# K cache rows of 8 KB with two batches interleaved by partition, and a reciprocal moved ahead of an output sum, in a cached attention kernel

## Chip, cores, metric

One core of a Trainium2 chip. The metric is device time in microseconds (us) of one execution; a lower time is better. A profile comes from one execution; its span, from the first instruction to the last, is some 1.8 us shorter than the device time. Every run quoted as fast ran in the undisturbed state.

## The reference

Two independent blocks A and B of the same shape; the outputs are put side by side.

```python
B, Sq, D = 16, 64, 640;  H, Sk, Dh = 32, 512, 128        # all bfloat16
q = (x @ wq).reshape(B, Sq, H, Dh).transpose(0, 2, 1, 3)
scores = einsum("bhqd,bhkd->bhqk", q, k_cache) * Dh ** -0.5
p = softmax(scores)
o = einsum("bhqk,bhkd->bhqd", p, v_cache)
out = o.transpose(0, 2, 1, 3).reshape(B, Sq, H * Dh) @ wo
```

K and V together are 268 MB and are read once. That makes the kernel a contest between transfers (about 406 GB/s in the profile below) and TensorE (90% busy).

## The kernel before

The work is cut into 128 steps. One step is a group of four heads for a pair of batches. (Where a number of bytes stands with it, a "step of 4 bytes", the word means something else: the distance in memory between two neighbouring columns that a matmul reads.) In each step two loads bring K, one per batch, 128 rows of 4 KB, one for each partition (lane) of the on-chip memory; VectorE transposes K in 32 x 32 blocks of 4-byte elements (pairs of bf16; one transpose of 128 x 1024 elements takes 1.24 us); TensorE multiplies q with it (the score matmuls: q is loaded as weights, K is the moving operand, 512 columns of it in each matmul), ScalarE takes the exp with row sums, VectorE the reciprocal, GpSimd normalises, TensorE transposes the weights, multiplies with V and with wo. Every fourth step VectorE takes over the output of four steps (the output sum: a copy in one half of the cases, an addition in the other). Each engine runs a list sorted by the numbers in `AT`.

```python
kn_ring = sb("kn_ring", [128, NK, 2, 2048], BF16)            # slot, batch, 16 keys x 128
kt_ring = sb("kt_ring", [128, NKT, 2, 16, 2, 32, 2], BF16)   # slot, batch, t, j, key row, pair
...
def em_LDK(e, op):                                            # one batch b of step n
    src = blocks[blk][1][2 * bp + b, h:h + 4].rearrange("h (p t) d -> (h p) (t d)", t=16)
    ins = e.dma_start(kn_ring[:, n % NK, b, :], src)
def em_KT(e, op):
    dst = kt_ring[:, n % NKT, b].rearrange("p t j k two -> p (t j k two)").bitcast(F32)
    ins = e.transpose(dst, kn_ring[:, n % NK, b, :].bitcast(F32))
def em_S(e, op):                                              # 4 x 2 x 4 = 32 matmuls
    for f in range(4):
        for b in range(2):
            for i in range(4):                                # head i in rows 32i..32i+31
                rows = slice(32 * i, 32 * i + 32)
                e.matmul(ps[64 * b:64 * b + 64, i, :], qs_ring[rows, n % NQ, f, b, :],
                         kt_ring[rows, n % NKT, b, :, f // 2, :, f % 2], ...,
                         tile_position=(32 * i, 64 * b))
```

The innermost index of the transposed K is the pair, so a score matmul picks every second bf16: a step of 4 bytes.

## Time and profile before

| | before |
|---|---|
| time, median of 3 | 759.53 us |
| TensorE busy | 682.2 us, 90% |
| VectorE busy | 536.7 us, 71% |
| transfers in the steady part | about 406 GB/s |
| steps 4 to 35 | 21.10 us per four steps |

The prediction reads the main views. Two more rows, of the costliest groups of the kernel before (line, engine, operation, output and inputs with shapes, count; then busy us, mean ns of one; then idle time before them), are needed for the comparison:

```profile
L610 DVE STREAM_TRANSPOSE kt_ring<-kn_ring 128x1024 f32<-128x1024 f32 x256 | 313.6, 1236 | 105.8 <-DMA kn_ring<-in_B_k_cache_dram 70.3
...
L620 PE MATMUL ps<-kt_ring,qs_ring 32*64 32x512 bf16 x4096 | 146.4, 396 | 0.0
```

The score matmuls overlap (the program places them on eight tiles of the array, and 32 of them, 396 ns each, are through in 1.14 us), so the busy time, 146.4 us for 128 steps or 1.14 us a step, is the number to watch, and not the 396 ns of one.

### The profile page before, as it was taken

To read this page: it belongs to the slowest core of one execution; us is meant where nothing else is said; L and a number is where in the kernel's file an instruction comes from. 1 tells how busy PE (TensorE), PEld (TensorE's weight loads), DVE (VectorE), ACT (ScalarE), POOL (GpSimd) and SP (SyncE) were. 2 spreads that over 40 slices of the span, in tenths; PEclk is the share of its full clock that TensorE was granted. 3 is DMA by queue.
4 is the path that set the end of the run, shared out by engine and by line. 5 is a ranking of instruction groups with operands and counts; after the bars stand their busy time and mean duration, and the time that the engine had idled before them with its cause. 6 is when DMAs were issued, how large, how long until landed. Compare 5 with 4: busy or idle time off the path is not lost.

```text
span 757.4 us, 57362 instructions
## 1 busy us (share of the span) xinstructions
PE 682.2 (90%) x26518; PEld 528.0 (70%) x26518; DVE 536.7 (71%) x818; ACT 519.6 (69%) x1559; POOL 404.6 (53%) x580
## 2 busy tenths in 40 slices
PE   4579999999999989999978999899997999999995
PEld 3457777777777767777756776677775777777773
DVE  7437777877767777687756777777675787887873
ACT  2437777777777677767756777777775677777772
POOL 5434555546864544645674455445486556455550
PEclk9979999999999999999999999999999999999997
DMA  8999999999999999999999999999999999999970
GB/s 309 394 399 405 406 406 407 406 405 407 400 395 409 407 408 406 407 407 407 406 394 401 406 407 407 406 405 405 406 403 395 406 408 407 402 409 406 407 294 16
DMA packets 99804, 295.12 MB, mean 390 GB/s; under 512 B 9264, under 2 KB 24112, under 8 KB 99760
## 3 DMA queue, kind: packets, MB, share of 16 engines
q1 hardware_dynamic: 91120, 284.20, 95.7%
q10 hardware_dynamic: 8640, 10.49, 3.8%
q14 instruction: 35, 0.29, 0.1%
q8 instruction: 9, 0.15, 0.1%
HBM read 292.03 MB, written 2.62 MB: 389 GB/s over the span
## 4 chain that ended last, share of the span: by engine, by line
PE 33%; SPq 26%; DMA 19%; POOL 9%; DVE 8%; issue 5%; ACT 0%; POOLq 0%; DVEq 0%; ACTq 0%
SPq L546 12%; POOL pn_sb L670 8%; SPq L557 8%; PE ps L705 8%; PE ps L725 8%; PE ps L597 7%; DMA kn_ring<-in_B_k_cache_dram 6%; PE ps L620 6%; DMA kn_ring<-in_A_k_cache_dram 5%; PE ps L681 5%; SPq L559 5%; DMA v_ring<-in_B_v_cache_dram 5%; DVE pT_sb L691 3%; DMA v_ring<-in_A_v_cache_dram 3%; DVE kt_ring L610 1%
## 5 line engine op out<-in xcount | busy, mean ns | idle before, releaser
L670 POOL TENSOR_SCALAR pn_sb<-p_ring,recip 128x512 bf16<-128x512 bf16 x508 | 342.3, 694 | 322.9 <-DVE recip L654 322.8
L610 DVE STREAM_TRANSPOSE kt_ring<-kn_ring 128x1024 f32<-128x1024 f32 x256 | 313.6, 1236 | 105.8 <-DMA kn_ring<-in_B_k_cache_dram 70.3
L641 ACT ACTIVATE p_ring<-ps 128x512 bf16<-128x512 f32 x512 | 298.7, 598 | 32.1 <-PE ps L620 20.3
L691 DVE COPY pT_sb<-ps 128x1024 bf16<-128x1024 bf16 x258 | 164.6, 679 | 79.5 <-PE ps L681 78.8
L705 PE MATMUL ps<-pT_sb,v_ring 32*128 32x64 bf16 (+1 forms) x14528 | 156.7, 192 | 26.2 <-DMA v_ring<-in_B_v_cache_dram 11.0
L725 PE MATMUL ps<-wo_sb,oT_sb 128*128 128x320 bf16 x1040 | 166.6, 303 | 5.9 <-issue 4.8
L597 PE MATMUL ps<-xT_ring,wqp_sb 128*128 128x128 bf16 x2560 | 166.0, 220 | 6.1 <-POOL xT_ring L586 5.8
L705 PEld LDWEIGHTS ps<-pT_sb,v_ring 32*128 32x128 bf16 (+1 forms) x14528 | 142.1, 92 | 40.6 <-DMA v_ring<-in_B_v_cache_dram 14.1
L597 PEld LDWEIGHTS ps<-xT_ring,wqp_sb 128*128 128x128 bf16 x2560 | 157.4, 114 | 13.0 <-issue 6.0
L713 ACT ACTIVATE oT_sb<-ps 128x256 bf16<-128x256 f32 x260 | 85.6, 381 | 107.0 <-PE ps L705 107.0
L620 PE MATMUL ps<-kt_ring,qs_ring 32*64 32x512 bf16 x4096 | 146.4, 396 | 0.0
L603 ACT ACTIVATE qs_ring<-ps 128x512 bf16<-128x512 f32 x128 | 76.5, 598 | 87.7 <-PE ps L597 87.6
L681 PEld LDWEIGHTS ps<-ident,pn_sb 64*128 64x128 bf16 x4128 | 70.8, 95 | 86.8 <-ACT ps L717 65.6
L725 PEld LDWEIGHTS ps<-wo_sb,oT_sb 128*128 128x128 bf16 x1040 | 91.9, 98 | 43.8 <-issue 5.4
L681 PE MATMUL ps<-ident,pn_sb 64*128 64x64 bf16 x4128 | 84.0, 191 | 26.4 <-POOL pn_sb L670 19.8
L641 ACT ACTIVATION_READ_ACCUMULATOR p_ring<-ps 128x1 f32 x512 | 105.9, 207 | 0.0
L620 PEld LDWEIGHTS ps<-kt_ring,qs_ring 32*64 32x64 bf16 x4096 | 55.1, 104 | 31.3 <-issue 0.5
L654 DVE RECIPROCAL recip<-rowsum 128x3 f32<-128x3 f32 (+1 forms) x256 | 36.1, 158 | 24.5 <-ACT p_ring L641 21.2
L717 ACT ACTIVATE ps<-zeros 128x256 f32<-128x256 bf16 x130 | 51.3, 395 | 0.0
L569 POOL COPY wqp_sb<-ws_sb 128x1280 bf16<-128x1280 bf16 x32 | 39.3, 1260 | 7.5 <-DMA ws_sb<-in_A_wq_dram 7.5
L586 POOL COPY xT_ring<-xs_sb 128x640 bf16<-128x640 bf16 x32 | 23.0, 720 | 3.6 <-PE ps L597 3.6
L576 PE MATMUL ps<-ident,xn_ring 128*128 128x128 bf16 x165 | 14.9, 222 | 4.7 <-DMA xn_ring<-in_A_x_dram 3.5
(26 smaller groups left out, 66.3 us busy)
## 6 DMA issues: line engine op xcount, KB each, us to landing
kn_ring<-in_A_k_cache_dram SPq DMA_DIRECT2D x128, 512.0 KB, 14.1
v_ring<-in_A_v_cache_dram SPq DMA_DIRECT2D x128, 512.0 KB, 13.0
kn_ring<-in_B_k_cache_dram SPq DMA_DIRECT2D x128, 512.0 KB, 15.1
v_ring<-in_B_v_cache_dram SPq DMA_DIRECT2D x128, 512.0 KB, 12.7
ws_sb<-in_B_wq_dram SPq DMA_DIRECT2D x10, 512.0 KB, 15.6
wo_sb<-in_B_wo_dram ACTq DMA_DIRECT2D x8, 640.0 KB, 10.9
ws_sb<-in_A_wq_dram SPq DMA_DIRECT2D x4, 640.0 KB, 10.1
wo_sb<-in_A_wo_dram SPq DMA_DIRECT2D x4, 640.0 KB, 12.5
```

Of the source, the lines that this page charges most:

```text
L546: ins = e.dma_start(kn_ring[:, n % NK, b, :], src)
L597: last = e.matmul(ps[:, 1, f * 128:(f + 1) * 128], w[:, kt, f, :], xT_ring[:, xs, kt, :], start=(kt == 0), stop=(kt == KT - 1))
L603: ins = e.activation(qs_ring[:, op.idx % NQ].rearrange("p f b q -> p (f b q)"), ps[:, 1, :], ACTF.Copy, scale=scale)
L610: ins = e.transpose(dst, kn_ring[:, n % NK, b, :].bitcast(F32))
L620: last = e.matmul(ps[64 * b:64 * b + 64, i, :], qs_ring[rows, n % NQ, f, b, :], kt_ring[rows, n % NKT, b, :, f // 2, :, f % 2], start=(f = ...
L641: ins = e.activation(dst, src, ACTF.Exp, scale=1.0, accum_out=rowsum[:, h:h + 1])
L670: ins = e.tensor_scalar(dst, src, recip[:, h // 4 % NR, i:i + 1], 1.0, ALU.mult, ALU.mult)
L681: last = e.transpose(pt_bank(b)[:, 64 * c:64 * c + 64], pn_sb[rows, c, :], ident[rows, rows], tile_position=(64 * b, 0))
L691: ins = e.tensor_copy(pT_sb[:, b].rearrange("p t q -> p (t q)"), pt_bank(b))
L705: last = e.matmul(ps[:, 4 + i, 64 * b:64 * b + 64], v_ring[rows, n % NV, b, c, :], pT_sb[rows, b, c, :], start=(t == 0 and i < 2), stop=(t ...
L713: ins = e.activation(oT_sb[:, 2 * a:2 * a + 2, :], o_ps[:, 2 * a:2 * a + 2, :], ACTF.Copy)
L725: last = e.matmul(out_ps[:, s, :], oT_sb[:, i, :], wo_sb[:, 4 * j + i, s * NH0:(s + 1) * NH0], start=(j == 0 and i == 0), stop=(j == NJ - ...
```

## The change

Its intent: half as many rows for K, each twice as long, so that the transfers pay half as many fixed costs (an estimate of 12 ns a packet, from the means in the trace of before: 87.9 ns for 2048 B and 163.6 ns for 4096 B). A batch of four heads is then only 64 rows. To keep head i in partitions 32i to 32i+31 for both batches, batch 0 goes to the even partitions and batch 1 to the odd ones. A transposed block therefore has the batches side by side, and the key order of the scores changes, which the exp undoes. Both transposes of a step now wait for both loads, and the second load stands in its list at the time of the first. The second part moves one reciprocal ahead of the output sum.

```diff
-              TE=(1.26, 1.39), ..., OS=2.53, ...
+              TE=(1.26, 1.39), ..., OS=2.545, ...
...
-            add("dve", "KT", (n, b), tk, [("kn", n % cfg.NK, b)], [("kt", n % cfg.NKT, b)])
+            add("dve", "KT", (n, b), tk, [("kn", n % cfg.NK, 0), ("kn", n % cfg.NK, 1)], [("kt", n % cfg.NKT, b)])
-            op = add("sp", "LDK", (n, b), tk - 0.9, [], [("kn", n % cfg.NK, b)])
+            op = add("sp", "LDK", (n, b), n + AT["KT"][0] - 0.9, [], [("kn", n % cfg.NK, b)])
...
-        kt_ring = sb("kt_ring", [128, NKT, 2, 16, 2, 32, 2], BF16)
+        kt_ring = sb("kt_ring", [128, NKT, 32, 2, 16, 2, 2], BF16)
...
-            src = blocks[blk][1][2 * bp + b, h:h + 4].rearrange("h (p t) d -> (h p) (t d)", t=16)
-            ins = e.dma_start(kn_ring[:, n % NK, b, :], src)
+            src = blocks[blk][1][2 * bp + b, h:h + 4].rearrange("h (p t) d -> (h p) (t d)", t=32)
+            dst = kn_ring[b::2, n % NK].rearrange("p a c -> p (a c)")
+            ins = e.dma_start(dst, src)
...
-                                        kt_ring[rows, n % NKT, b, :, f // 2, :, f % 2],
+                                        kt_ring[rows, n % NKT, :, f // 2, :, b, f % 2],
...
-            if h // 4 % NJ in WIDE:
-                return src, dst
-            return (src.rearrange("q (th tl k) -> q tl k th", th=2, tl=8), ...)
+            u = 2 if h // 4 % NJ in WIDE else 4
+            return (src.rearrange("q (u t p) -> q t p u", u=u, p=16), dst.rearrange("q (t p u) -> q t p u", p=16, u=u))
```

With the batch between key row and pair, the score matmuls' step becomes 8 bytes.

More of the change, by code (lines that the diff above doesn't have):

```diff
@@ L32 @@
               EX=(0.21, 0.32, 0.43, 0.54), RC=(0.53, 0.75), NM=(0.56, 0.69, 0.82, 0.95), NMZ=(0.54, 0.55, 0.56, 0.76), TR=1.2,
-              TE=(1.26, 1.39), PV=1.75, OE=(2.0, 2.06), ZO=2.11, OP=2.31, OS=2.53, LDWO=2.6, ST=3.374, WP0=-1.75, WP1=-1.6)
+              TE=(1.26, 1.39), PV=1.75, OE=(2.0, 2.06), ZO=2.11, OP=2.31, OS=2.545, LDWO=2.6, ST=3.374, WP0=-1.75, WP1=-1.6)
 class Op:
@@ L607, in em_KT @@
         def em_KT(e, op):
-            n, b = op.idx
-            dst = kt_ring[:, n % NKT, b].rearrange("p t j k two -> p (t j k two)").bitcast(F32)
-            ins = e.transpose(dst, kn_ring[:, n % NK, b, :].bitcast(F32))
+            n, a = op.idx
+            dst = kt_ring[:, n % NKT, 16 * a:16 * a + 16].rearrange("p t j k b two -> p (t j k b two)").bitcast(F32)
+            ins = e.transpose(dst, kn_ring[:, n % NK, a, :].bitcast(F32))
             return ins, ins
@@ L632, in exp_views @@
             src, dst = ps[:, h % 4, :], p_ring[:, h % NP, :]
-            if h // 4 % NJ in WIDE:
-                return src, dst
-            return (src.rearrange("q (th tl k) -> q tl k th", th=2, tl=8),
-                    dst.rearrange("q (tl k th) -> q tl k th", tl=8, th=2))
+            u = 2 if h // 4 % NJ in WIDE else 4
+            return (src.rearrange("q (u t p) -> q t p u", u=u, p=16), dst.rearrange("q (t p u) -> q t p u", p=16, u=u))
         def em_EX(e, op):
```

## The prediction

The sum: 2.8 + 6.6 + 1.9 + 0.5 = 11.8 us, so 747.7 us, and 748.7 with one microsecond given back. Rival (a): loads of 64 rows into every second partition are slower in themselves.

> **What bounds the kernel now.** I read the page's tenths first, then the windows view over stretches, the waits inside each stretch, and the timeline of one group of four steps. A step is one group of four heads for two batches; there are 128 (the page's 256 transposes, two a step).
>
> ```profile
> PE   4579999999999989999978999899997999999995
> PEclk9979999999999999999999999999999999999997
> DMA  8999999999999999999999999999999999999970
> GB/s 309 394 399 405 406 406 407 406 405 407 400 395 409 407 408 406 407 407 407 406 394 401 406 407 407 406 405 405 406 403 395 406 408 407 402 409 406 407 294 16
> ...
> q1 hardware_dynamic: 91120, 284.20, 95.7%
> ```
>
> The transfers never rest: about 406 GB/s from the third slice to the thirty-eighth. TensorE is at 90% or more in nearly all of them too, at full clock. So two limits lie close together, and the averages do not say which holds where. The starts of the score matmuls (L620) in the timeline do. Steps 4 to 35 (55.8 to 225 us) repeat 5.09, 5.48, 5.44, 5.09 us, 21.10 us per four steps, like clockwork. Steps 36 to 103 (225 to 616 us) are irregular, 391 us for 17 groups of four, 23.0 us each. Steps 104 to 127 are regular again, 21.17 us per four. The windows view over these stretches:
>
> ```profile
> 55.70:225.00 169.30, 166.02 (x6580) 129.57 (x6568) 125.99 (x198) 130.32 (x390) 100.03 (x143) 1.00 1.03 404
> 225.00:616.00 391.00, 355.25 (x13968) 274.99 (x13957) 279.10 (x426) 273.70 (x824) 213.64 (x306) 1.00 1.03 405
> 616.00:742.00 126.00, 122.92 (x4849) 95.33 (x4839) 97.92 (x149) 94.42 (x287) 66.32 (x99) 1.00 0.96 379
> ```
>
> TensorE is busy 98% (166.0 of 169.3), 91% and 98% (122.9 of 126.0). The waits agree. In the middle stretch VectorE waits 96.5 us for K:
>
> ```profile
> DVE kt_ring L610 <- DMA kn_ring<-in_B_k_cache_dram: 65.2, 52, 3.9
> DVE kt_ring L610 <- DMA kn_ring<-in_A_k_cache_dram: 31.3, 34, 2.4
> ```
>
> In the first regular stretch that wait is 0.6 us, and the queue of loads waits for TensorE to free V buffers instead:
>
> ```profile
> SPq L557 <- PE ps L705: 39.9, 21, 3.9
> SPq L559 <- PE ps L705: 22.5, 8, 3.3
> ```
>
> So the middle is set by transfers and the two outer stretches by TensorE. The transfers have little to spare in the first: 404 GB/s there is their pace in the middle.
>
> Why does one step of the regular four take 5.44 and not 5.09? The timeline shows that step and the one after it:
>
> ```profile
> 150.70 1.14 PE L620 MATMUL ps<-kt_ring,qs_ring 32*64 32x512 bf16 x32
> ...
> 152.11 0.64 PE L681 MATMUL ps<-ident,pn_sb 64*128 64x64 bf16 x32 [0.27 <-POOL pn_sb L670]
> ...
> 156.14 1.14 PE L620 MATMUL ps<-kt_ring,qs_ring 32*64 32x512 bf16 x32
> ...
> 157.21 0.64 PE L681 MATMUL ps<-ident,pn_sb 64*128 64x64 bf16 x32
> ...
> 169.38 0.81 DVE L735 COPY acc<-ps 128x640 f32<-128x640 f32 x1
> ...
> 170.11 0.21 DVE L654 RECIPROCAL recip<-rowsum 128x3 f32<-128x3 f32 x2
> ...
> 170.37 2.03 POOL L670 TENSOR_SCALAR pn_sb<-p_ring,recip 128x512 bf16<-128x512 bf16 x3 [3.02 <-DVE recip L654]
> ```
>
> At 152.11 TensorE idled 0.27 us for GpSimd's normalisation; at 157.21 it started 0.07 us before the score matmuls were through. 0.27 + 0.07 is the 0.35 us. The cause stands in the last three lines, the same place one group later: the output sum (L735, 0.81 us) goes ahead of the reciprocal on VectorE, so normalisation begins late. (The 5.48 step has the five extra x transposes, 0.44 us of real work.)
>
> [...] The trace's records of single packets on q1 agree: 87.9 ns mean for 2048 B (16,384 of them), 163.6 ns for 4096 B (59,264), so 75.7 ns per 2 KB and 12.1 ns fixed. [...] The score matmul now steps 4 bytes through K[...]; its 32 matmuls take 1.14 us. The trace has no moving operand at 8 bytes.
>
> **The change, part by part.**
> - *K rows.* A K load of 512 KB is 128 rows of 4 KB now, 64 rows of 8 KB after, into the even or the odd partitions. From the two packet sizes I estimate an 8 KB packet at 163.6 + 2 x 75.7 = 315 ns. Per load: 128 x 163.6 = 20.94 us of one engine against 64 x 315 = 20.16, a saving of 0.78, over 16 engines 0.049 us. Eight K loads per four steps: 0.39 us. All 256 loads: 12.5 us, which is the most that fewer packets can give.
> - *The transposes* keep their count, shape and 1.24 us. But both now wait for both loads; the first used to run while the second load landed (the two start 1.28 us apart where data binds). That is about 1.15 us more from the last landing to the end of transposing. With a median of 13 to 15 us from issue to landing (page, part 6), a deep queue stands ahead of the transfer engines; a later release of a slot shortens it and does not empty it. I count 0 in the steady state.
> - *Score matmuls* read K at a step of 8 bytes[...]. I count 0, with a risk below.
> - *Exp* reads PSUM in 2 or 4 interleaved runs. A quarter of the exps already read two runs at a 256-element step: 597.4 ns against 597.6 for the plain ones. 0.
> - *The reciprocal.* The instruction order shows the reciprocal of three heads ahead of the output sum, that of the fourth behind it. The reciprocal's data are ready at 169.42 (third accumulator read) and VectorE is free at 169.46, so it starts some 0.65 us earlier. The wait of 0.35 us goes; 20.75 us per four steps is left for TensorE. The output sum ends 0.2 us later, at about 170.4, still before the value matmuls at 170.65 that overwrite its bank.
>
> The sum by stretch. First regular: TensorE needs 20.75 for 21.10, and the transfers save 0.39, so both limits move: 8 groups x 0.35 = 2.8 us. Middle: 17 x 0.39 = 6.6 us. Last: 24 steps less the tail, 5.5 groups x 0.35 = 1.9 us. Start-up (to 55.8 us, set by loads): about 16 K loads x 0.049 = 0.8, less some of the later transposing, 0.5 us. Together 11.8 us, 759.5 - 11.8 = 747.7. Since neither limit has slack over the other once both moved, I give one microsecond back: **748.7 us**.
>
> **Rivals.**
> (a) [...] 15% for a loss above 2%.
> (b) *The wider step slows the score matmuls.* TensorE is the bound in 40% of the time. The weight loads of L597, which step 8 bytes, take a median 113 ns against 98 for contiguous ones (L725) of equal shape. A tenth more on 1.14 us is 0.11 us a step, 0.46 per four: it cancels the reciprocal's gain and leaves TensorE at 21.2; the time would be about 753 to 756 us. 20%.
> (c) *Only one part works.* If 4 KB rows were limited by memory and not by packets, only the reciprocal counts: 2.8 + 1.9, about 755 us. The straight line through two packet sizes speaks against it. 10%.
> (d) *The later transposes bite* in the middle, where VectorE waits for K and then copies the transposed weights in order: if the queue is shallower than I read, up to 1 us in some of 68 steps, which takes back much of the 6.6 us.
>
> **Range and chances.** With neither (a) nor (b), 744 to 752. Over 2% faster means under 744.3, which needs more than the 12.5 us of packets, or the reciprocal helping in the middle too: 12%. Over 2% slower is above 774.7 and comes nearly only from (a), plus a little for a strong (b): 16%. The rest, 72%, is within 2%. The range runs from 743.5 to 768, its upper end holding (b), (c), (d) and a mild (a).
>
> **What would show it.** Packets on q1 fall by 16,384 to 74,736; single 8 KB packets last 310 to 320 ns (over 400: rival a). GB/s rises from 406 to about 413 in the middle. The regular four becomes 5.09, 5.48, 5.09, 5.09 and TensorE's idle time for normalisation (19.8 us in 44 waits) falls below 8. Thirty-two score matmuls stay at 1.14 us (over 1.2: rival b). VectorE's waits for K shrink or stay near 100 us; above 150 speaks for (d). A time over 775 us would make the whole account wrong.

## The result, and the profile after

The changed kernel takes 820.75 us (median of 4) against 759.12 for before (median of 4): a ratio of 1.0809, interval 1.079 to 1.0828, so 8.1% slower. Ratios here are the mean time of one kernel's fast runs over the mean of the other's of the same rounds, so not quite the ratio of the medians quoted. The clock was 0.989 in the profiled run.

The same rows of the page of the changed kernel, the tenths and the transfer rate over the 40 slices, the queue, the chain that ended last, and the two groups:

```profile
PE   4689999999999999999999999999999999999995
...
GB/s 318 399 406 409 404 370 346 355 359 338 366 399 411 395 369 374 381 366 365 365 387 405 411 403 386 361 363 380 351 367 400 399 360 354 363 353 348 346 170 14
...
q1 hardware_dynamic: 74736, 284.20, 91.3%
...
PE 96%; issue 2%; DVE 1%; ACT 0%; DVEq 0%
...
L611 DVE STREAM_TRANSPOSE kt_ring<-kn_ring 128x1024 f32<-128x1024 f32 x256 | 302.9, 1222 | 1.0 <-DMA kn_ring<-in_A_k_cache_dram 1.0
L621 PE MATMUL ps<-kt_ring,qs_ring 32*64 32x512 bf16 x4096 | 261.1, 620 | 0.0
```

The last row is the finding. The same 4096 score matmuls are busy for 261.1 us in place of 146.4, and one lasts 620 ns in place of 396. TensorE is at 9 tenths without a gap, the final chain is 96% TensorE, and the transfers have fallen back to 340 to 410 GB/s because the loads wait for TensorE. The waits of the load queue for TensorE show it: over the whole run 464.5 us in these two rows of the changed kernel, against 85.3 us in the same two rows of before (54.9 + 30.4, whole-run view).

```profile
SPq L558 <- PE ps L704: 347.7, 92, 6.5
SPq L560 <- PE ps L704: 116.8, 31, 5.0
```

VectorE's wait for K, 96.5 us in the middle stretch before, is 1.0 us in the whole run (the row of L611 above). One step of the timeline of the changed kernel, the one with the output sum in it (start, duration, engine, line):

```profile
401.26 2.06 PE L621 MATMUL ps<-kt_ring,qs_ring 32*64 32x512 bf16 x32
...
403.25 0.64 PE L680 MATMUL ps<-ident,pn_sb 64*128 64x64 bf16 x32
...
405.33 0.17 DVE L653 RECIPROCAL recip<-rowsum 128x3 f32<-128x3 f32 x1
405.42 0.81 DVE L737 TENSOR_TENSOR out_sb<-acc,ps 128x640 bf16<-128x640 f32 x1
405.60 2.70 POOL L669 TENSOR_SCALAR pn_sb<-p_ring,recip 128x512 bf16<-128x512 bf16 x4 [3.21 <-DVE recip L653]
...
407.55 2.07 PE L621 MATMUL ps<-kt_ring,qs_ring 32*64 32x512 bf16 x32
```

Thirty-two score matmuls take 2.06 us where they took 1.14. The second part of the change does what it was meant to: the reciprocal is ahead of the output sum and GpSimd starts 0.27 us after it, but nothing waits for it any more.

**Where the 61.5 us are** (spans 818.9 and 757.4, from the starts of the score matmuls in the two timelines). Start-up to step 4: 56.9 against 55.7, +1.2. Steps 4 to 35: 193.3 against 169.3, +24.0. Steps 36 to 103: 411.1 against 391.0, +20.1. The rest: 157.6 against 141.4, +16.2. Four steps now take 24.17 us from step 8 to the end, with hardly a deviation. The score matmuls alone are busy for 261.1 - 146.4 = 114.7 us more, 0.90 us a step on average (2.06 - 1.14 = 0.92 in the step shown). TensorE as a whole is busy for 787.6 - 682.2 = 105.4 us more, as the score matmuls overlap a little with their neighbours. Of these, 61.5 us show in the span; the other 43.9 filled idle time of TensorE, 35.7 of them in the middle stretch (391.0 - 355.3), where it is now busy throughout.

### The profile page after: what moved, and what is told of

It is laid out like the page before. It is cut to its first block, busy times and chain, and to the rows that moved or that the text cites. A ratio compares the mean times of both kernels' runs of the same rounds, so it can differ in the third digit from the quotient of the medians.

```text
span 818.9 us, 57490 instructions
## 1 busy us (share of the span) xinstructions
PE 787.6 (96%) x26518; PEld 535.3 (65%) x26518; DVE 533.9 (65%) x818; ACT 520.2 (64%) x1559; POOL 405.5 (50%) x580
## 3 DMA queue, kind: packets, MB, share of 16 engines
q1 hardware_dynamic: 74736, 284.20, 91.3%
## 4 chain that ended last, share of the span: by engine, by line
PE 96%; issue 2%; DVE 1%; ACT 0%; DVEq 0%
PE ps L621 31%; PE ps L724 19%; PE ps L704 18%; PE ps L598 18%; PE ps L680 9%; PE ps L577 1%; DVE v_ring L509 0%; DVE pT_sb L690 0%; DVE kt_ring L611 0%; DVE ps L513 0%; ACT oT_sb L712 0%; DVE pT_sb L688 0%; DVE out_sb L737 0%; ACT ps L716 0%; DVE wo_sb L517 0%
## 5 line engine op out<-in xcount | busy, mean ns | idle before, releaser
L640 ACT ACTIVATE p_ring<-ps 128x512 bf16<-128x512 f32 x512 | 298.7, 598 | 139.6 <-PE ps L621 122.4
L690 DVE COPY pT_sb<-ps 128x1024 bf16<-128x1024 bf16 x258 | 166.3, 686 | 222.2 <-PE ps L680 222.2
L611 DVE STREAM_TRANSPOSE kt_ring<-kn_ring 128x1024 f32<-128x1024 f32 x256 | 302.9, 1222 | 1.0 <-DMA kn_ring<-in_A_k_cache_dram 1.0
L621 PE MATMUL ps<-kt_ring,qs_ring 32*64 32x512 bf16 x4096 | 261.1, 620 | 0.0
L704 PEld LDWEIGHTS ps<-pT_sb,v_ring 32*128 32x128 bf16 (+1 forms) x14528 | 141.3, 92 | 19.8 <-issue 8.6
L680 PEld LDWEIGHTS ps<-ident,pn_sb 64*128 64x128 bf16 x4128 | 67.8, 95 | 119.0 <-ACT ps L716 115.7
L621 PEld LDWEIGHTS ps<-kt_ring,qs_ring 32*64 32x64 bf16 x4096 | 65.3, 113 | 76.7 <-issue 71.1
L653 DVE RECIPROCAL recip<-rowsum 128x3 f32<-128x3 f32 (+1 forms) x256 | 43.2, 169 | 51.8 <-ACT p_ring L640 38.4
## 6 DMA issues: line engine op xcount, KB each, us to landing
wo_sb<-in_B_wo_dram ACTq DMA_DIRECT2D x8, 640.0 KB, 11.6
```

The lines of the kernel that those rows point to most:

```text
L611: ins = e.transpose(dst, kn_ring[:, n % NK, a, :].bitcast(F32))
L621: last = e.matmul(ps[64 * b:64 * b + 64, i, :], qs_ring[rows, n % NQ, f, b, :], kt_ring[rows, n % NKT, :, f // 2, :, b, f % 2], start=(f = ...
L640: ins = e.activation(dst, src, ACTF.Exp, scale=1.0, accum_out=rowsum[:, h:h + 1])
L680: last = e.transpose(pt_bank(b)[:, 64 * c:64 * c + 64], pn_sb[rows, c, :], ident[rows, rows], tile_position=(64 * b, 0))
L690: ins = e.tensor_copy(pT_sb[:, b].rearrange("p t q -> p (t q)"), pt_bank(b))
L704: last = e.matmul(ps[:, 4 + i, 64 * b:64 * b + 64], v_ring[rows, n % NV, b, c, :], pT_sb[rows, b, c, :], start=(t == 0 and i < 2), stop=(t ...
```

## Experiments

The theory after the result: the step of 8 bytes in the score matmuls' moving operand makes the loss, and everything else in the sum holds. Rivals: the two batches' matmuls, which run side by side, disturb each other when their columns alternate in memory, as they do in the changed kernel; or the new shape of the loads and the later transposes cost something too. Scores of this input are tiny, the softmax is nearly flat, and the comparison with the reference lets a wrong key order through. Followed through load, transpose, score matmul and exp, the key order of the changed kernel, e5, e7 and e8 comes out as in the kernel before.

### e1: the reciprocal alone

```diff
 (kernel before)
-OS=2.53
+OS=2.545
```

> The kernel before with the reciprocal moved ahead of the output sum and nothing else. If the wait of TensorE for GpSimd in the step after an output sum (0.35 us, once in four steps) goes where TensorE sets the pace, the regular four steps take 20.75 us in place of 21.10 and the time falls by 4.7 us, to about 755 (ratio 0.994). Rival: the wait only moves (another operation starts as late), the four steps stay at 21.1 and the time at 759.

Measured: 757.92 us against 759.0, ratio 0.9989 (0.9972 to 1.0006): the same. The view of waits of TensorE shows that the mechanism works. Waits for the normalisation fall from 44 to 30 in the whole run:

```profile
PE ps L681 <- POOL pn_sb L670: 11.6, 30, 0.6
```

The regular four steps take 20.87 us (5.00, 5.58, 5.09, 5.20) in place of 21.10: 0.35 us go in the step that waited and 0.1 in the first, 0.1 come back in each of the two others. Step 32 starts at 201.6 in place of 203.4. But steps 32 to 35 then take 23.89 us in place of 21.60, and step 36 starts at 225.5 against 225.0: the lead is gone. The transfers ran at 405 GB/s up to step 32, their full pace of this kernel; TensorE had only drawn on the loads queued ahead, and then waited for them (2.5 us for V in two waits). What TensorE gains in a stretch is lost when the transfers are as close behind as here.

### e2: the rows alone

```diff
 (changed kernel)
-OS=2.545
+OS=2.53
```

> The changed kernel with the old order of reciprocal and output sum. Theory: the score matmuls, now 2.06 us in place of 1.14, end so late that the normalisation is never waited for, so this part of the change is worth nothing beside the rows: 820 to 821 us. Rival: it still carries its 0.35 us per four steps over the whole run, then some 11 us more: about 832.

Measured: 820.64 us, ratio 1.0814 (1.0796 to 1.0832), the same as the changed kernel. TensorE's waits no longer contain the normalisation. The slow score matmuls hide the second part of the change altogether; the whole loss is in the first.

### e3: the changed kernel with score matmuls at 4 bytes (wrong)

```diff
-    kt_ring[rows, n % NKT, :, f // 2, :, b, f % 2],
+    kt_flat[rows, n % NKT, 2048 * b + 1024 * (f // 2) + f % 2:2048 * b + 1024 * (f // 2) + 1024:2],
```

> Wrong result on purpose: the changed kernel, but the score matmuls read each batch's half of the buffer at a step of 4 bytes, as before; transfers, transposes and waits are those of the changed kernel. If only the score matmuls' reading made the loss, 32 of them take 1.14 us again and the prediction's sum for everything else holds: about 748 us. If the transposes' later start[...] cost something as well, the time lies between 755 and 820.

Measured: 750.64 us against 759.0, ratio 0.989 (0.9874 to 0.9907). Only the reading of one operand differs from the changed kernel, and the 70 us between 820.75 and 750.64 go with it. (It reads 2 KB without a gap, where the kernel before reads runs of 128 bytes in every 256; its score matmuls are busy for 3.0 us less than those of before. Up to that much of the gain of e3, and of e9 below, may be theirs.) The transfer rate over the slices and the row of the score matmuls of this run:

```profile
GB/s 317 398 402 411 412 410 414 412 410 413 407 398 414 413 413 413 414 412 414 412 400 406 411 411 411 413 410 411 412 409 398 411 413 413 409 412 414 407 259 15
...
L623 PE MATMUL ps<-kt_ring,qs_ring 32*64 32x512 bf16 x4096 | 143.4, 392 | 0.0
```

The rate rises from about 406 GB/s to between 409 and 414 in most slices, so the longer rows do what they were made for. The trace's records of single packets give 315.7 ns as the mean of 16,384 packets of 8192 B (the prediction's estimate was 315; two packets of 4096 B took 2 x 163.6 = 327.2 ns in the kernel before).

### e9: as e3, with the old order on VectorE (wrong)

```diff
 (e3)
-OS=2.545
+OS=2.53
```

> Wrong result on purpose: the changed kernel with score matmuls at a step of 4 bytes and the old order of reciprocal and output sum, so the rows alone without their cost to TensorE. The reciprocal alone gave 1.1 us, both together 8.4. If the two parts simply add, the rows are worth 7.3: 751.7 us. If TensorE's pace caps the rows' gain in the regular stretches (21.1 us per four steps instead of 20.8), the rows give 5 to 6 us: 753 to 754 us.

Measured: 751.39 us against 758.75, ratio 0.9896 (0.9877 to 0.9915). The rows alone, without their cost to TensorE, are worth 7.4 us; the reciprocal adds 0.7 in e3, within the spread of the runs. The parts add up, and the rows are nearly all of it. The starts of the score matmuls in the three traces (one execution each) show where:

| us | before | e9 (rows) | e3 (rows and reciprocal) |
|---|---|---|---|
| start-up to step 4 | 55.7 | 57.2 | 56.9 |
| steps 4 to 35 | 169.3 | 168.8 | 167.0 |
| steps 36 to 103 | 391.0 | 383.2 | 385.9 |
| the rest | 141.4 | 140.4 | 139.6 |

The rows gain 7.8 us in the middle, where the transfers set the pace. Against e9, the reciprocal in e3 gains 1.8 us in the stretch before it, and the middle takes that back; in e1 it was lost already in steps 32 to 35.

### e4: the kernel before with score matmuls at 8 bytes (wrong)

```diff
-    kt_ring[rows, n % NKT, b, :, f // 2, :, f % 2],
+    kt_flat[rows, n % NKT, 2048 * b + f:2048 * b + 2048:4],
```

(Theory 2 is the first rival above: the two batches disturb each other where their columns alternate in memory. In e4 they do not alternate.)

> Wrong result on purpose: the kernel before, all as it was, but the score matmuls step 8 bytes through the 4 KB of their own batch[...]. Theory 1 (the step of 8 bytes alone halves the reading): 32 score matmuls take 2.06 us, the time is about 820 us. Theory 2 (it is the two batches' matmuls, running side by side[...]): 1.14 us and 759 us.

Measured: 813.65 us (two runs) against 759.12, ratio 1.0721 (1.0681 to 1.076). Here rows, transposes and order are those of before, and each batch reads its own 4 KB, so the columns of the two do not alternate. The loss is nearly complete all the same:

```profile
L622 PE MATMUL ps<-kt_ring,qs_ring 32*64 32x512 bf16 x4096 | 254.7, 622 | 0.0
```

The step itself is enough: 254.7 us busy against 146.4. Alternating columns are not needed. The 7.1 us to the changed kernel go with score matmuls that are busy for 6.4 us less; e4 reads without gaps, the changed kernel in runs of 128 bytes.

### e6: the disputed cost by itself

After the end of the kernel before, with nothing else running, eleven sets of score-like matmuls of 512 columns, one code line for each set (one execution; the first set, L831, only warms up). This shows the line for the changed kernel's case:

```diff
+    for f in range(4):
+        for b in (0, 1):
+            for i in range(4):
+                rows = slice(32 * i, 32 * i + 32)
+                e.matmul(ps[64 * b:64 * b + 64, i, :], qs_ring[rows, 1, f, b, :],
+                         kn_flat[rows, 2 * b + f % 2 + 2048 * (f // 2):2 * b + f % 2 + 2048 * (f // 2) + 2048:4], ...)
```

(In the expectation, the set at 8 bytes "as the changed kernel" has the columns of the two batches alternating, and only there did theory 2 expect 2.0 us. Cut with the words on how the memory is read is a third case: if the two batches add up at the reading side, one batch alone takes no longer at 8 bytes than at 4.)

> The kernel before with score-like matmuls added after its end, nothing else on the chip: 4 x 2 x 4 matmuls of 512 columns as in the score step, eight times over, at steps of 2, 4, 8 and 16 bytes with the two batches in regions of their own, at 4 bytes with both at the same addresses, at 8 bytes[...] (as the changed kernel), and at 4, 8 and 16 bytes with the matmuls of one batch alone. Theory 1: per 32 matmuls 1.1 us at 2 and 4 bytes, 2.0 at 8, 2.0 or more at 16, apart or shared; Theory 2: 1.1 at every step while apart[...].[...]

The groups by line, in the stretch after the kernel's end (busy us for 256 matmuls, then the mean ns of one):

```profile
L903 PE MATMUL ps<-kn_ring,qs_ring 32*64 32x512 bf16 x256 | 58.4, 1074 | 0.0
L895 PE MATMUL ps<-kn_ring,qs_ring 32*64 32x512 bf16 x256 | 29.7, 626 | 0.0
L879 PE MATMUL ps<-kn_ring,qs_ring 32*64 32x512 bf16 x256 | 29.6, 1077 | 0.0
L887 PE MATMUL ps<-kn_ring,qs_ring 32*64 32x512 bf16 x256 | 15.3, 383 | 0.0
L871 PE MATMUL ps<-kn_ring,qs_ring 32*64 32x512 bf16 x256 | 15.2, 630 | 0.0
L863 PE MATMUL ps<-kn_ring,qs_ring 32*64 32x512 bf16 x256 | 15.1, 628 | 0.0
...
L911 PE MATMUL ps<-kn_ring,qs_ring 32*64 32x512 bf16 x256 | 10.0, 417 | 0.0
L855 PE MATMUL ps<-kn_ring,qs_ring 32*64 32x512 bf16 x256 | 7.8, 384 | 0.0
L847 PE MATMUL ps<-kn_ring,qs_ring 32*64 32x512 bf16 x256 | 7.7, 385 | 0.0
L839 PE MATMUL ps<-kn_ring,qs_ring 32*64 32x512 bf16 x256 | 7.2, 374 | 0.0
```

Divided by eight, per 32 matmuls of two batches:

| step | busy us per 32 | line |
|---|---|---|
| 2 bytes, batches apart | 0.90 | L839 |
| 4 bytes, apart | 0.96 | L847 |
| 4 bytes, same addresses | 0.98 | L855 |
| 8 bytes, apart | 1.89 | L863 |
| 8 bytes, columns of the two batches alternating, as in the changed kernel | 1.90 | L871 |
| 16 bytes, apart | 3.70 | L879 |

From 2 bytes to 4 the step is nearly free (0.90 against 0.96 us); the time doubles at 8 bytes (1.89) and again at 16 (3.70). Apart or alternating makes no difference (1.89 against 1.90). With one batch alone (L887, L895, L903: steps 4, 8, 16) the same number of matmuls takes 15.3, 29.7 and 58.4 us, twice as long as with two (7.7, 15.1 and 29.6), as only the tiles of one batch are in use; the ratio between the steps is the same (29.7 to 15.3 is 1.94, 15.1 to 7.7 is 1.96). So the two batches do not add up at the reading side, and it is the distance that one matmul's operand advances per column which counts. The theory's number for one step, 2.06 - 1.14 = 0.92 us, is 1.90 - 0.96 = 0.94 here. The granted clock was 1.00 in the sets of the table and in L887 and L895. It fell to 0.50 from about 890 us on, in L903, whose ratio to L895 (1.97) is nevertheless that of L879 to L863 (1.96).

The eleventh set, L911, was not in the expectation: a step of 4 bytes in runs of 64 bytes out of every 256, as in e7 below. Its 10.0 us overstate it, since it starts at the low clock and among the last matmuls of L903; from 944.13 us on the timeline has 201 of its matmuls in 5.95 us, 0.95 us per 32, as fast as without gaps.

### e5: transposes that write the batches apart

If the step is the fault, the batches must lie apart in the transposed K. The transpose can write so: element by element to alternating places 4 KB from each other.

```diff
 (changed kernel)
-kt_ring = sb("kt_ring", [128, NKT, 32, 2, 16, 2, 2], BF16)
+kt_ring = sb("kt_ring", [128, NKT, 2, 32, 2, 16, 2], BF16)
...
-dst = kt_ring[:, n % NKT, 16 * a:16 * a + 16].rearrange("p t j k b two -> p (t j k b two)").bitcast(F32)
+dst = kt_ring[:, n % NKT, :, 16 * a:16 * a + 16].rearrange("p b t j k two -> p b (t j k two)").bitcast(F32).rearrange("p b c -> p c b")
...
-    kt_ring[rows, n % NKT, :, f // 2, :, b, f % 2],
+    kt_ring[rows, n % NKT, b, :, f // 2, :, f % 2],
```

> Correct result wanted: 8 KB rows as in the changed kernel, but the transposes write the two batches apart (16 keys of one batch side by side, the other batch's 4 KB further on), so the score matmuls step 4 bytes inside their own batch. If the transpose takes 1.24 us whatever its writing order, about 748 us and faster than both kernels. Rival: writing pairs 4 KB apart doubles a transpose to 2.5 us; VectorE then needs some 7 us a step and the time is about 900 us.

Measured: 755.61 us against 759.0, ratio 0.9962 (0.9945 to 0.9979): correct and faster than both kernels, though by 0.4% only. The score matmuls are back at 150.0 us busy, but neither expectation on the transpose was right:

```profile
L611 DVE STREAM_TRANSPOSE kt_ring<-kn_ring 128x1024 f32<-128x1024 f32 x256 | 496.2, 2019 | 14.3 <-DMA kn_ring<-in_B_k_cache_dram 14.1
```

A transpose takes 2.02 us in place of 1.22. VectorE is then busy for 692.6 of 752.3 us, and a regular group of four steps takes 21.60 us, against 20.79 in e3. Between 60 and 205 us VectorE is busy for 142.4 of 145.0 us, TensorE for 139.8: the loss has moved from TensorE to VectorE and become smaller.

### e7: batches 64 bytes apart

```diff
 (changed kernel)
-kt_ring = sb("kt_ring", [128, NKT, 32, 2, 16, 2, 2], BF16)
+kt_ring = sb("kt_ring", [128, NKT, 32, 2, 2, 16, 2], BF16)
...
+dst = kt_ring[:, n % NKT, 16 * a:16 * a + 16].rearrange("p t j b k two -> p (t j b k two)").bitcast(F32).rearrange("p (tj b k) -> p tj k b", b=2, k=16)
...
+    kt_ring[rows, n % NKT, :, f // 2, b, :, f % 2],
```

> 8 KB rows with the batches 64 bytes apart: each transpose writes 16 keys of one batch, then 16 of the other, inside one 128-byte block. If a transpose's cost comes from the distance between neighbouring writes, 64 bytes may cost less than the 4 KB of the split version (2.02 us): at 1.24 us VectorE is no bound and the time is 750 to 752 us. If any non-contiguous write costs the same, 2.0 us again and 755 to 757 us. The score matmuls read runs of 64 bytes in every 256 and may take 1.2 to 1.4 us.

Measured: 753.86 us against 758.75, ratio 0.9931 (0.9914 to 0.9949), the lowest ratio of the correct versions (its interval overlaps those of e5 and e8). The transpose is hardly better (1.95 us, against 2.02 in e5 with writes 4 KB apart), so the distance of the writes matters little; the score matmuls, which I had expected to slow down, take 1.09 us a step and are the fastest of all versions. The set L911 of e6 agrees that runs of 64 bytes cost nothing (0.95 us per 32, against 0.96 without gaps). Why they read a little faster than the runs of 128 in the kernel before (1.14) stays open.

```profile
L611 DVE STREAM_TRANSPOSE kt_ring<-kn_ring 128x1024 f32<-128x1024 f32 x256 | 478.5, 1946 | 25.2 <-DMA kn_ring<-in_B_k_cache_dram 21.2
...
L621 PE MATMUL ps<-kt_ring,qs_ring 32*64 32x512 bf16 x4096 | 139.8, 384 | 0.0
```

### e8: three groups of four split, the fourth in 4 KB rows

```diff
 (e5)
+if j not in WIDE:
+    src = blocks[blk][1][2 * bp + b, h:h + 4].rearrange("h (p t) d -> (h p) (t d)", t=16)
+    ins = e.dma_start(kn_ring[:, n % NK, b, :], src)
... (transpose, score matmul and exp of such a group as in the kernel before)
```

> The split version for three groups of heads in four; the fourth keeps 4 KB rows, contiguous transposes and the old views. VectorE loses 2 x 0.78 = 1.56 us per four steps, 21.6 becomes about 20.1, below TensorE's 20.8; the transfers keep three quarters of their saving (0.29 us per four). About 751 to 753 us, faster than before and than the split version (755.6).

Measured: 754.82 us against 758.75, ratio 0.9957 (0.9933 to 0.9982), no better than e5 (0.9962). A regular four steps do fall from 21.60 to 21.23 us, but not to 20.8. The trace says why. TensorE alone is busy for 20.81 us of the 21.23 (steps 8 to 31), against 20.58 in e3, whose score matmuls read without gaps. Once in four steps it also waits some 0.4 us for the normalisation (2.2 us in six waits between 60 and 205 us): the reciprocal comes late on VectorE, which still has transposes of 2.02 us in three steps of four. So the load of VectorE in single steps counts, not only its mean over four; no run tested this last point.

## Why the prediction was wrong

It said 748.7 us and 72% for "within 2%"; the time is 820.75, far outside the range. Its own closing sentence named the mark: over 775 us the whole account is wrong. It is not quite the whole account, and the experiments say which step failed.

- **The step that failed** is the one on the score matmuls at a step of 8 bytes: "I count 0". No trace had shown that, as the prediction itself noted. The runs put 0.92 us a step in its place, 0.90 on average (e6: 0.94 by itself; e4: nearly the whole loss with nothing else changed; e3: all of it gone with the step back at 4 bytes). On TensorE, which the prediction itself had found 98% busy in two stretches of three, 0.92 us in about 5.3 could not be hidden.
- **Rival (b) was the right mechanism** and was mis-sized: a tenth more on 1.14 us, from a comparison of weight loads, 753 to 756 us. It measured 78% more (146.4 to 261.1 us busy), and its own mark, over 1.2 us for 32 score matmuls, was passed by far (2.06). The weight loads at 8 bytes (113 against 98 ns, 15% more) told nothing about a moving operand. The prediction had noted that the trace held no moving operand at 8 bytes, and should have let the range follow from that, as a doubling of the reading would have been one line of working: 128 x 1.14 = 146 us more on TensorE, less its idle time.
- **The rows** were right: q1 fell by 16,384 packets to 74,736, an 8 KB packet took 315.7 ns in e3 against 315 estimated, and without the slow matmuls the rows alone gave 7.4 us (e9). The prediction had 6.6 for the middle and 0.5 for the start-up; the trace of e9 has 7.8 in the middle, and a start-up that is 1.5 us longer.
- **Rival (a), slower loads of 64 rows,** did not come: its mark was packets of 8 KB over 400 ns. In the changed kernel their mean is 328 and their median 309 ns; in e3 the mean is 315.7, at 409 to 414 GB/s in most slices.
- **The reciprocal** was right in its mechanism (0.35 us in the waiting step) and wrong in its worth. The sum had 4.7 us for it; alone it gave 1.1, not clear of the noise (e1), and the waits for the normalisation fell from 19.8 us to 11.6 there and 12.4 in e3, not below 8. The term left out that TensorE's gain in a regular stretch is only an advance on loads that do not come sooner. In the changed kernel it is worth nothing (e2).
- **The later transposes** were counted as 0 in the steady state and as a little at the start. In the middle they show no cost: e9 has them too and takes 383.2 us for steps 36 to 103, where the sum had 391.0 - 6.6 = 384.4 (e3 takes 385.9; it reaches step 36 with a lead of 2.2 us over e9, from the reciprocal for the most part, and has lost it by step 104), and VectorE waits there 82.1 us for K in place of 96.5, so rival (d) did not come. At the start the sum had the sign wrong: step 4 begins at 56.5 to 57.5 us in the seven traces with rows of 8 KB and at 55.3 to 55.7 in the three without (before, e1, e4). Whether the later transposes or the longer rows make that, no run took apart.
- **Transposes unchanged, exp unchanged:** right. 1.22 against 1.24 us and 598 against 598 ns (means of the pages).
- The sum for all of this without the slow matmuls was 747.7 us; e3 measured 750.64.
- One reading was a little too smooth: the groups of steps 32 to 35 and 108 to 111 took 21.60 and 21.62 us, not 21.10 and 21.17. Nothing hangs on it.

## What to carry to other kernels

When a layout change makes transfers cheaper, look at the step with which every later engine reads the new layout, and measure a new step on the busiest engine before anything else; a test of a few matmuls behind the end of the old kernel settles it (e6 gave 0.94 us a step, the changed kernel 0.92). Where two limits lie as close together as TensorE and the transfers here, a gain on one is worth what the other has to spare (e1: 1.1 us of the 4.7 counted), and a cost on either shows as soon as its own slack is used up (105.4 us more on TensorE, of which its idle time took 43.9). And a comparison with the reference that passes is no proof of an index order, if the data make the result insensitive to it.
